# Seed stores from GpSimd's queue, and the first attention unit's key maxima by pairs with a second set of key differences

## The chip, the cores and the metric

The kernel runs on one core of a Trainium2 chip. A core has a matrix engine (PE, with its weight loads PEld), a vector engine (DVE), a scalar engine (ACT), GpSimd (POOL) and a queue engine that only issues transfers (SP), and 16 DMA engines that all queues share. The metric is the device time of one execution in microseconds, the median of several runs.

## The reference

Two independent halves, side by side in the output. Half A is a long convolution (S4D) over 2048 positions and 448 channels, with a kernel that is a sum of 256 exponentials for each channel. Half B is full softmax attention with 16 heads of 28.

```python
# A: u [1, 2048, 448]
dt = exp(log_dt);  A = -exp(log_A_real) + 1j * A_imag;  C = (C_real + 1j * C_imag) * dt[:, None]
K = 2 * real(einsum("dn,dnl->dl", C, exp((A * dt[:, None])[:, :, None] * arange(L))))
a = irfft(rfft(u_t, 2 * L) * rfft(K, 2 * L))[..., :L] + u * D_skip
# B: x [1, 2048, 448]
q, k, v = split(x @ wqkv)                       # 16 heads of 28
b = (softmax(q k^T * 28 ** -0.5) v) @ wo
out = concatenate([a, b], -1)                   # [1, 2048, 896]
```

All data is float32.

## The kernel before

**Attention.** The 16 heads are four groups (`G`) of four (`HG`), and the queries four chunks (`NQ`) of 512 (`CQ`). A unit is one group and one chunk, so there are 16. Queries and keys are split into a high and a low part, so that one product over 128 rows (four times 32) stands for a product of full precision. The projection writes these parts to DRAM: `q_d` for queries, `k_d` for keys, `v_d` for values. `load_q` brings one unit's queries back as the tile `qhat` (four loads of 32 partitions), and `load_k` one head's keys as `khat` (four loads of 32 partitions by 2048).

**The maxima.** A unit needs each query's largest score before its exponentials. `max_mm(u, i, kc)` handles one of 16 tiles `i` (a head `j` and 128 queries) in four steps `kc`, each a product of 128x512 into a PSUM tile. Step 0 multiplies with the differences `kd_g`, first half of a block of keys less the second half, for the key chunks 0 and 1; ACT takes the relu (tile `rl`). Step 1 multiplies with the second halves of these blocks, and DVE adds `rl` and takes the maximum in one operation, since max(a, b) = relu(a - b) + b. So two steps cover 1024 keys. Steps 2 and 3 multiply with key chunks 2 and 3, and DVE takes a plain maximum of 512 scores each. `max_join` takes the largest of the three parts, and `max_end` and `max_put` write the negated maxima into spare rows of `qhat`. Unit 0's maxima stand alone ahead of the main loop, with five PSUM tiles in turn (`more`). In the main loop the maxima of a later unit run beside the current unit's scores and exponentials.

**The first stage.** A list of slots `t` interleaves two things. Each call of `project` runs one projection job: 128 query or key rows of a group (`qk_proj`) or values (`v_proj`). Its evacuation follows one job later (`evac`), and for keys in chunks 0 and 1 it also makes the differences (`kb`, `dhl`) and stores them in `kd_d`. The other thing is the seeds: eight rounds `o` of `seeds(o)`, a pipeline over ACT, DVE and POOL that makes the first powers of the exponentials for half A. A round ends with two stores, `put_g` (tile `sg`, 1456 KB) and `put_e` (896 KB, in a `qhat` buffer), issued by SP. The pool of `qhat` has three buffers, for seeds and queries alike. `ahead` holds loads for the first unit by slot: from slot `A0` = 26 on the differences of group 0 (16 loads of 64 KB), and from `A1` = 34 on the queries of unit 0 (two slots, two loads each). After slot 36 (`PW` = 37) the projection's weights are released. In that space the keys of group 0 are loaded, heads 0 and 1 from ACT's queue and 2 and 3 from SP's, and then unit 1's queries and group 0's values from SP's. Then come unit 0's maxima.

**Order.** A planner orders the instructions of the first part by dependences and priorities; from the main loop on the program's order is kept. Each engine and each queue runs its own list in order. A load or store waits in its queue for its data and for its buffer, and what is behind it on that queue waits too.

**The main loop** runs 16 units of 16 steps, with half A's work in slots between. It loads the differences of later groups by `load_kd`, and the seeds by `load_sd`.

All engine instructions carry line 75 in the profile, a helper that records every operation, so the views are read by tile names.

## Time and profile before

| | us |
|---|---|
| median of three runs | 1360.99 |
| lowest and highest | 1358.85, 1361.72 |
| the profiled execution, its own time | 1363.72 |
| its span, first to last instruction | 1361.9 |
| mean granted TensorE clock | 0.976 |

Busy in that span: PE 1243.9 (91%), DVE 991.3 (73%), ACT 966.1 (71%), POOL 839.5 (62%). The DMA queues moved 205.36 MB, a mean of 151 GB/s. All of it went through SP's queue (201.13 MB) and ACT's (2.10 MB), beside 2.13 MB of instructions; POOL issued none.

A group's row in the profile reads: engine, operation, out<-in, partitions x elements, count | busy us, mean ns of one | idle us of the engine just before them, and what ended it. The chain of waits is a list of start, length and what the end depended on. A tile's row reads: engine, operation, count: shortest/median/longest ns, first and last start. SPq, ACTq stand for an engine's queue; a row of a transfer there is its issue, not its movement. A row of waits reads: who <- for whom: us in total, times, longest.

### The profile page before, as it was taken

The numbers are of one execution on the slowest core, as the hardware profiler recorded it, in microseconds if no ns is written. First come the engines' busy times: TensorE is split into PE (matmuls) and PEld (weight loads), VectorE is DVE, ScalarE is ACT, GpSimd is POOL, SyncE is SP. The second block draws the span as 40 slices with busy tenths as digits, with TensorE's granted clock in tenths as the row PEclk, the third lists the DMA queues.
The fourth block names the chain that finished last, engine by engine and source line by source line (L and its number), as shares of the span: only waits on it lengthen the run. The fifth ranks groups of instructions, "written<-read, shape, count | busy, mean of one in ns | idle before, by whom it ended". The sixth has DMA issues, their size and how long they took to land.

```text
span 1361.9 us, 33142 instructions
## 1 busy us (share of the span) xinstructions
PE 1243.9 (91%) x12625; PEld 709.8 (52%) x12625; DVE 991.3 (73%) x2138; ACT 966.1 (71%) x2067; POOL 839.5 (62%) x705
## 2 busy tenths in 40 slices
PE   6878885799999999999999999999998999998997
PEld 5657762455555555555555555555555545544433
DVE  5897886877777777777788888888887766857311
ACT  4876752488888888888888887878786655655553
POOL 3685681278877878878888988888895111202221
PEclk9988987899999999999999999999999999999999
DMA  6677669636675545378534233632325534636476
GB/s 197 199 261 266 225 212 271 179 74 150 147 164 118 128 135 159 111 202 198 162 94 97 56 73 86 146 79 67 79 65 140 189 116 161 206 111 203 138 192 176
DMA packets 200089, 205.36 MB, mean 151 GB/s; under 512 B 95993, under 2 KB 158521, under 8 KB 197881
## 3 DMA queue, kind: packets, MB, share of 16 engines
q1 hardware_dynamic: 199544, 201.13, 53.2%
q10 hardware_dynamic: 384, 2.10, 0.6%
q8 instruction: 100, 1.64, 0.5%
q14 instruction: 61, 0.49, 0.1%
HBM read 120.73 MB, written 82.18 MB: 149 GB/s over the span
## 4 chain that ended last, share of the span: by engine, by line
PE 61%; DVE 17%; ACT 12%; issue 3%; DMA 3%; POOL 3%; SPq 0%; ACTq 0%; DVEq 0%; POOLq 0%
PE pm L75 35%; PE po L75 13%; PE pss L75 12%; ACT p L75 6%; DVE mx L75 4%; DVE g L75 2%; DVE tri L75 2%; ACT rl L75 2%; DVE p L75 2%; POOL qhat L75 1%; DVE pr L75 1%; DVE zg L75 1%; DVE rl L75 1%; DVE sg L75 1%; ACT tri L75 1%
## 5 line engine op out<-in xcount | busy, mean ns | idle before, releaser
L75 ACT ACTIVATE p<-pss 128x512 f32<-128x512 f32 x1024 | 565.4, 609 | 138.5 <-PE pss L75 127.5
L75 PE MATMUL pss<-qhat,khat 128*128 128x512 f32 x1024 | 403.1, 400 | 3.3 <-ACT p L75 3.3
L75 DVE TENSOR_REDUCE mx<-pm 128x1 f32<-128x512 f32 x500 | 321.4, 683 | 116.3 <-PE pm L75 115.1
L75 PE MATMUL pm<-khat,qhat 128*128 128x512 f32 x749 | 330.1, 444 | 41.4 <-DVE mx L75 36.5
L75 POOL TENSOR_TENSOR e<-e,sdb 128x256 f32<-128x256 f32 x168 | 201.8, 1201 | 171.9 <-ACT e L75 162.9
L75 PE MATMUL po<-p,v 128*32 128x512 f32 x2048 | 271.9, 599 | 0.0
L75 POOL TENSOR_TENSOR e<-e,eu 128x256 f32<-128x256 f32 x168 | 248.1, 1477 | 13.2
L75 PEld LDWEIGHTS pm<-khat,qhat 128*128 128x128 f32 x749 | 142.0, 190 | 216.0 <-DVE mx L75 79.8
L75 PEld LDWEIGHTS pss<-qhat,khat 128*128 128x128 f32 x1024 | 191.1, 189 | 46.7 <-ACT p L75 11.2
L75 DVE CUSTOM_DVE_ANT_0 rl<-pm,rl 128x512 f32<-128x512 f32 x249 | 171.4, 688 | 48.3 <-ACT rl L75 43.8
L75 POOL TENSOR_TENSOR eu<-e,sdb 128x256 f32<-128x256 f32 x168 | 201.7, 1201 | 0.0
L75 DVE TENSOR_TENSOR g<-g,zg 128x128 f32<-128x128 f32 x392 | 162.9, 416 | 46.3 <-ACT zg L75 41.3
L75 ACT ACTIVATE rl<-pm 128x512 f32<-128x512 f32 x249 | 151.2, 607 | 20.7 <-PE pm L75 18.8
L75 POOL TENSOR_TENSOR p<-pr,pr 64x448 f32<-64x448 f32 x32 | 40.9, 1277 | 191.6 <-DVE pr L75 180.5
L75 PE MATMUL pm<-kdif,qhat 128*128 128x512 f32 x249 | 101.6, 408 | 2.2 <-DVE mx L75 1.5
L75 PEld LDWEIGHTS pm<-e,g 128*32 128x32 f32 x3584 | 63.0, 110 | 52.8 <-issue 30.8
L75 DVE TENSOR_TENSOR zg<-g,zg 128x128 f32<-128x128 f32 x224 | 87.5, 391 | 1.9
L75 PEld LDWEIGHTS po<-p,v 128*32 128x32 f32 x2048 | 56.6, 110 | 42.7 <-issue 38.0
L75 PE MATMUL pm<-xh,wh 112*128 112x512 f32 x128 | 56.8, 448 | 22.3 <-DVE hl L75 10.8
L75 PE MATMUL pm<-e,g 128*32 128x64 f32 x3584 | 72.5, 220 | 0.0
L75 ACT ACTIVATE y<-pm 128x448 f32<-128x448 f32 x48 | 26.3, 548 | 63.0 <-PE pm L75 30.7
L75 DVE TENSOR_TENSOR pr<-pm,ub 128x448 f32<-128x448 f32 x64 | 37.0, 619 | 32.7 <-PE pm L75 32.7
(137 smaller groups left out, 1571.8 us busy)
## 6 DMA issues: line engine op xcount, KB each, us to landing
sdb<-sd SPq DMA_DIRECT2D x56, 336.0 KB
qhat<-q SPq DMA_DIRECT2D x64, 256.0 KB
khat<-k SPq DMA_DIRECT2D x56, 256.0 KB
sd<-sg SPq DMA_DIRECT2D x8, 1456.0 KB
k<-hl SPq DMA_DIRECT2D x16, 512.0 KB
q<-hl SPq DMA_DIRECT2D x16, 512.0 KB
mw<-in_mw SPq DMA_DIRECT2D x16, 512.0 KB
sd<-qhat SPq DMA_DIRECT2D x8, 896.0 KB
```

The costliest lines, as they stand in the source:

```text
L75: i = f(*args, **kw)
```

## The change

- `put_e` and `put_g` are issued by GpSimd instead of SP, and so are the four loads of unit 1's queries, which moves them behind the last slot; the values' loads move there too and stay on SP.
- Unit 0's maxima run in pairs on both halves of the keys: step 2 is a product with a second set of differences (chunks 2 and 3) and a relu, step 3 the product with the second halves and the fused add and maximum. The join takes two parts instead of three. `rl` has three buffers there.
- The second differences are made in the evacuation for group 0 and chunks 2 and 3 (two jobs), stored in a new DRAM tile `kd2`, and loaded by SP (four loads of 256 KB) into a new pool `k2_p` before the keys of heads 2 and 3.
- The first differences of a group share one tile `kdif`; those of group 0 are loaded by four loads of 256 KB in slots 27 to 30, and unit 0's queries in slots 25 and 26.

Other units keep their three parts.

```diff
--- before.py
+++ after.py
@@ -41,7 +41,7 @@
 PS = 1
 SGB, XB, XL = 2, 5, 4
 K0, KP, KD, UP = 0, 3.5, 5, 3
-A0, A1 = 26, 34
+A0, A1 = 27, 25
 
 N1 = 32
 N2 = 64
@@ -103,6 +103,7 @@
     dram = ctx.enter_context(tc.tile_pool(name="dram", bufs=1, space=DRAM))
     k_d = [dram.tile([2, 128, L], F32, name=f"k_{g}") for g in range(G)]
     kd_d = [dram.tile([2, 128, CQ], F32, name=f"kd_{g}") for g in range(G)]
+    kd_d.append(dram.tile([2, 128, CQ], F32, name="kd2"))
     q_d = [[dram.tile([2, 128, CQ], F32, name=f"q_{g}_{c}") for c in range(NQ)] for g in range(G)]
     sd_d = [dram.tile([BO, 128, SDF], F32, name=f"sd_{o}") for o in range(NO)]
     yu_d = dram.tile([128, N1, D], F32, name="yu_d")
@@ -152,35 +153,42 @@
         v_g[g, c] = t = v_p.tile([128, NK // NQ, HG, 32], F32, name="v", bufs=5)
         nc.sync.dma_start(t.rearrange("p t h e -> p t (h e)"), v_d[c][:, g])
 
-    def load_kd(g, j, rows=range(4)):
-        if 0 in rows:
-            kd_g[g, j] = kd_p.tile([128, CQ], F32R, name=f"kdif{j}")
-        t = kd_g[g, j]
-        for r in rows:
-            nc.sync.dma_start(t[32 * r:32 * r + 32].bitcast(F32), kd_d[g][r % 2, 32 * j:32 * j + 32, :])
-
-    def load_q(u, rows=range(4)):
+    kd_t = kd_p.tile([128, HG, CQ], F32R, name="kdif")
+
+    def load_kd(g, j):
+        kd_g[g, j] = kd_t[:, j, :]
+        for r in range(4):
+            nc.sync.dma_start(kd_t[32 * r:32 * r + 32, j, :].bitcast(F32), kd_d[g][r % 2, 32 * j:32 * j + 32, :])
+
+    def load_kd_row(r, g=0, t=kd_t):
+
+        kd_g.update({(g, j): t[:, j, :] for j in range(HG)})
+        nc.sync.dma_start(t[32 * r:32 * r + 32].bitcast(F32), kd_d[g][r % 2].rearrange("(j p) q -> p j q", j=HG))
+
+    def load_q(u, rows=range(4), queue=nc.sync):
         g, c = divmod(u, NQ)
         if 0 in rows:
             q_u[u] = q_p.tile([128, HG, CQ], F32R, name="qhat", bufs=3)
         t = q_u[u]
         for r in rows:
-            nc.sync.dma_start(t[32 * r:32 * r + 32].bitcast(F32), q_d[g][c][r // 2].rearrange("(j p) q -> p j q", j=HG))
-
-    def max_mm(u, i, kc, ps=w_tile):
+            queue.dma_start(t[32 * r:32 * r + 32].bitcast(F32), q_d[g][c][r // 2].rearrange("(j p) q -> p j q", j=HG))
+
+    def max_mm(u, i, kc, ps=w_tile, p2=None):
+
 
         if i == 0 and kc == 0:
             m_u[u] = q_p.tile([128, HG, 4, 3], F32, name="mx", bufs=2)
         j, t = divmod(i, 4)
         pm = ps()
         q, kt = q_u[u][:, j, t * 128:(t + 1) * 128], kt_g[u // NQ][j]
-        mx = m_u[u][:, j, t, max(kc - 1, 0):max(kc - 1, 0) + 1]
-        if kc == 0:
-            nc.tensor.matmul(pm, q, kd_g[u // NQ, j], start=True, stop=True)
-            rl_u[u, i] = kd_p.tile([128, CQ], F32, name="rl", bufs=2)
+        n = kc // 2 if p2 else max(kc - 1, 0)
+        mx = m_u[u][:, j, t, n:n + 1]
+        if kc == 0 or kc == 2 and p2:
+            nc.tensor.matmul(pm, q, kd_g[G if kc else u // NQ, j], start=True, stop=True)
+            rl_u[u, i] = (p2 or kd_p).tile([128, CQ], F32, name="rl", bufs=3 if p2 else 2)
             nc.scalar.activation(rl_u[u, i], pm, AF.Relu)
-        elif kc == 1:
-            kb = kt.rearrange("p (c s n) -> p c s n", c=NQ, s=2)[:, :2, 1, :]
+        elif kc == 1 or kc == 3 and p2:
+            kb = kt.rearrange("p (c s n) -> p c s n", c=NQ, s=2)[:, kc - 1:kc + 1, 1, :]
             nc.tensor.matmul(pm.rearrange("p (c n) -> p c n", c=2), q, kb, start=True, stop=True)
             rl = rl_u.pop((u, i))
             nc.vector.tensor_tensor_reduce(rl, pm, rl, 1.0, -3.0e38, ALU.add, ALU.max, mx)
@@ -188,9 +196,9 @@
             nc.tensor.matmul(pm, q, kt[:, kc * CQ:(kc + 1) * CQ], start=True, stop=True)
             nc.vector.tensor_reduce(mx, pm, axis=AX.X, op=ALU.max)
 
-    def max_join(u):
+    def max_join(u, n=3):
         m_u[u, 1] = q_p.tile([128, HG * 4], F32, name="m1", bufs=2)
-        nc.vector.tensor_reduce(m_u[u, 1], m_u[u].rearrange("p a b c -> p (a b) c"), axis=AX.X, op=ALU.max)
+        nc.vector.tensor_reduce(m_u[u, 1], m_u[u].rearrange("p a b c -> p (a b) c")[:, :, :n], axis=AX.X, op=ALU.max)
 
     def max_end(u, ps):
         nc.tensor.transpose(ps[:16, :128], m_u[u, 1], ident)
@@ -420,8 +428,8 @@
             e8 = lambda *i: sl(q["e8"], *i)
             e3 = lambda: cmul(vec if o % 8 < E3 else pol, e8(3, 4), e8(1, 2), 1, q["e8"][:, :, 0, :, 2], q["e8"][:, :, 1, :, 2], False)
             e5 = lambda: cmul(pol, e8(5, 8), e8(1, 4), 3, q["e8"][:, :, 0, :, 4], q["e8"][:, :, 1, :, 4], False)
-            put_e = lambda: nc.sync.dma_start(sd_d[o][:, :, :F_G].rearrange("b p f -> p b f"), q["se"])
-            put_g = lambda: nc.sync.dma_start(sd_d[o][:, :, F_G:].rearrange("b p f -> p b f"), q["sg"])
+            put_e = lambda: nc.gpsimd.dma_start(sd_d[o][:, :, :F_G].rearrange("b p f -> p b f"), q["se"])
+            put_g = lambda: nc.gpsimd.dma_start(sd_d[o][:, :, F_G:].rearrange("b p f -> p b f"), q["sg"])
 
             def load():
                 if o not in nats:
@@ -463,7 +471,7 @@
                 else:
                     nc.scalar.activation(th, pp, AF.Copy)
                     nc.vector.tensor_tensor(tl, pp, th.bitcast(F32), ALU.subtract)
-                if s == 1 and c < 2:
+                if s == 1 and (c < 2 or g == 0):
                     HC = CQ // 2
                     kb = y_p.tile([128, HC], F32, name="kb")
                     dhl = y_p.tile([128, 2, HC], F32R, name="dhl")
@@ -472,7 +480,7 @@
                     nc.vector.tensor_tensor(kb, pp[:, :HC], kb, ALU.subtract)
                     nc.scalar.activation(dh, kb, AF.Copy)
                     nc.gpsimd.tensor_tensor(dl, kb, dh.bitcast(F32), ALU.subtract)
-                    nc.sync.dma_start(kd_d[g][:, :, c * HC:(c + 1) * HC].rearrange("i p l -> p i l"), dhl.bitcast(F32))
+                    nc.sync.dma_start(kd_d[g if c < 2 else G][:, :, c % 2 * HC:(c % 2 + 1) * HC].rearrange("i p l -> p i l"), dhl.bitcast(F32))
                 nc.sync.dma_start((k_d[g][:, :, c * CQ:(c + 1) * CQ] if s == 1 else q_d[g][c]).rearrange("i p l -> p i l"),
                                   hl.bitcast(F32))
             return evac
@@ -511,8 +519,8 @@
         pend, n_work = [], len(work)
 
         ahead = collections.defaultdict(list)
-        for i in range(2 * HG):
-            ahead[A0 + i].append(lambda i=i: load_kd(0, i // 2, range(2 * (i % 2), 2 * (i % 2) + 2)))
+        for i in range(4):
+            ahead[A0 + i].append(lambda i=i: load_kd_row(i))
         for i in range(2):
             ahead[A1 + i].append(lambda i=i: load_q(0, range(2 * i, 2 * i + 2)))
 
@@ -533,17 +541,22 @@
                 project()
                 wst.close()
                 k0_p = pool(k0_st, "k0_p", side="right")
+                k2_p = pool(st, "k2_p", side="right")
                 for j in range(HG):
+                    if j == 2:
+                        k2_t = k2_p.tile([128, HG, CQ], F32R, name="kd2")
+                        for r in range(4):
+                            load_kd_row(r, G, k2_t)
                     load_k(0, j, k0_p, nc.scalar if j < 2 else nc.sync)
-                load_q(1)
-                for c in range(NQ):
-                    load_v(0, c)
+        load_q(1, queue=nc.gpsimd)
+        for c in range(NQ):
+            load_v(0, c)
         xst.close()
         more = [lambda: ps_t.tile([128, CQ], F32, name="pt")] * 2 + [w_tile] * 3
         for i in range(16):
             for kc in range(4):
-                max_mm(0, i, kc, more[(4 * i + kc) % 5])
-        max_join(0)
+                max_mm(0, i, kc, more[(4 * i + kc) % 5], k2_p)
+        max_join(0, 2)
         max_end(0, ps_t.tile([128, CQ], F32, name="pt"))
         max_put(0)
         sst.close()
```

## The prediction

> **What bounds the kernel now.** I read the page's row of PE in 40 equal slices first, then busy time by stage, then the chain of waits where the stages meet. A row by stage has its length, the busy time (and instructions) of PE, its weight loads, DVE, ACT and POOL, PE's granted clock, the DMA engines' share and GB/s.
>
> ```profile
> PE   6878885799999999999999999999998999998997
> ```
>
> One digit is 34 us. Up to slice 7 (to about 264 us) PE has gaps; from there to the end it is 9 of 10 or more busy. The change edits the part ahead of that. Whatever is won or lost before about 260 us therefore moves the rest as a block.
>
> ```profile
> 0.00:204.00 204.00, 165.40 (x705) 131.31 (x705) 161.00 (x284) 134.89 (x268) 131.80 (x156) 0.92 0.69 226
> 204.00:217.85 13.85, 0.31 (x3) 0.03 (x1) 3.45 (x7) 2.22 (x6) 3.77 (x4) 0.65 1.04 288
> 217.85:251.00 33.15, 26.06 (x64) 12.81 (x64) 29.48 (x65) 9.57 (x17) 0.00 (x0) 0.89 0.96 268
> ```
>
> Three stages. Projection and seeds (0 to 204): no engine is full, PE is at 81%, DVE 79%, ACT 66%, POOL 65%. A hole (204 to 217.85): only the DMA engines work, at a share of 1.04. Unit 0's maxima (217.85 to 251): DVE is at 89% and the DMA engines still at 0.96. The chain says what ends each:
>
> ```profile
> 204.11 6.44 DMA khat<-k
> ...
> 210.93 6.78 DMA qhat<-q
> ...
> 217.85 1.19 PE pt L75 x2
> ...
> 225.82 0.60 DVE rl L75
> 226.42 1.21 DVE mx L75 x3
> ...
> 249.55 1.22 DVE mx L75 x3
> ```
>
> The hole is two loads in a row: the first key tile, and then two rows of unit 0's queries, which SP issued only when that load had landed. After it DVE repeats 0.60 (the fused add and max, `rl`) and 1.21 (two plain maxima, with the read-out of the accumulator under the first): **1.81 us for one of 16 tiles**.
>
> **The change part by part.**
>
> *Maxima in pairs.* A tile's two plain maxima are replaced by a second relu on ACT and a second fused operation on DVE.
>
> ```profile
> L75 DVE TENSOR_REDUCE mx<-pm 128x1 f32<-128x512 f32 x20 | 13.1, 685 | 11.4 <-PE pm L75 11.4
> L75 DVE CUSTOM_DVE_ANT_0 rl<-pm,rl 128x512 f32<-128x512 f32 x9 | 6.1, 681 | 1.4 <-PE pm L75 1.4
> L75 ACT ACTIVATE rl<-pm 128x512 f32<-128x512 f32 x9 | 5.4, 597 | 11.7 <-PE pm L75 9.8 <-DVE mx L75 1.9
> ...
> 221.60:242.00 20.40, 16.24 (x43) 7.07 (x42) 20.07 (x46) 6.57 (x11) 0.00 (x0) 1.00 1.05 262
> ```
>
> A fused operation lasts as long as a plain maximum (681 against 685 ns), so DVE goes from three steps of 0.60 to two, 1.21 us a tile: 16 x 0.605 = **9.7 us less**. The cover: ACT needs 2 x 0.597 = 1.19 us a tile, just under DVE; PE issues four products a tile either way and was busy 16.24 of 20.40 us at full clock over about 11 tiles, by pipelined times that overlap. So ACT follows close behind: where a relu is late, DVE waits. With PE at the lower clock it would be PE (two products took 1.19 us from 217.85 on, so four take up to 2.4). Bounds: 9.7 (DVE paces) to 0 (keys or relus pace); I take 9.7, the nearest row's.
>
> *The start.* Unit 0's queries and key differences now load during the projection, in slots 25 to 30. The 16 loads of 64 KB for the differences become four of 256 KB. The query rows leave the hole, and the second set of differences comes into it: four loads of 256 KB, of the same form as the query rows, and all four are needed before tile 0's third product.
>
> ```profile
> SPq L75 <- DMA khat<-k: 19.2, 12, 8.8
> ...
> 207.12 9.75 ACTq L75 DMA_DIRECT2D khat<-k  x5
> ...
> 211.94 0.42 SPq L75 DMA_DIRECT2D sd<-qhat  x1
> ```
>
> SP waited 8.8 us once for a load of keys that ACT had issued, though what it was to issue did not read it. The new loads stand at the same place behind the same eight, so I expect the same wait to hit them: what ends last is a different load, at the same time. Bounds: they land with the first key tile (6.8 us earlier, the query row's length), or 0.52 MB more at 288 GB/s costs 1.8 us, doubled for a shared queue 3.6. The seeds' store of 0.92 MB that SP issued at 211.94 is no longer between; I take **0**. ACT issues keys until about 216.9 in any case, and its relus stand behind them.
>
> *Second differences.* Two more evacuations make one: two copies on ACT, a subtraction on DVE and one on POOL, and a store of 256 KB.
>
> ```profile
> L75 ACT ACTIVATE kb<-pm x8: 363/374/387, 23.5 to 100.9; 128x256 f32<-128x256 f32 x8
> L75 DVE TENSOR_TENSOR kb<-pm,kb x8: 404/417/426, 24.4 to 102.3; 128x256 f32<-128x256 f32 x8
> L75 ACT ACTIVATE dhl<-kb x8: 401/416/425, 24.8 to 102.8; 128x256 fp32r<-128x256 f32 x8
> L75 POOL TENSOR_TENSOR dhl<-kb,dhl x8: 740/1168/1932, 25.3 to 106.9; 128x256 fp32r<-128x256 f32 x8
> ...
>   PE pm L75: 6.4, 4
> ```
>
> Eight of them held PE up by 6.4 us (last row: who waited for the tile), 0.8 each: **+1.6** for two. Without cover each would be 0.37 + 0.42 + 0.42 + 1.17 = 2.4, so the bounds are 0 and 4.8.
>
> *The stores on POOL's queue.* 16 of them, 896 rows each (7 blocks by 128 partitions). SP's side, then what POOL has room for:
>
> ```profile
> L75 SPq DMA_DIRECT2D sd<-qhat x8: 360/513/1276, 60.7 to 237.7; - x8
> ...
> L75 POOL TENSOR_TENSOR gz<-tri 128x224 f32<-128x224 f32 x8 | 6.8, 850 | 20.1 <-ACT tri L75 19.2 <-DVE px L75 0.8
> L75 POOL TENSOR_TENSOR vl<-tri,vh 112x448 fp32r<-112x448 f32 x4 | 5.1, 1284 | 13.0 <-ACT vh L75 9.7 <-DMA pw<-in_pw 3.2
> ...
> by line: PE pm L75 14.6%; DVE tri L75 13.4%; POOL qhat L75 9.6%; issue 6.8%; DVE sg L75 6.0%; ACT tri L75 5.8%; DVE px L75 5.7%; DVE qhat L75 5.3%; POOL tri L75 4.4%; DMA tri<-in_B_wqkv 3.9%; DVE hl L75 3.2%; PE pt L75 2.2%; POOL x_e L75 2.
> ```
>
> No row shows a DMA issued by POOL. From below: 0, all of it in POOL's idle 204 - 131.8 = 72 us. A wait for ACT's and DVE's part of a seed stands in that queue too, and behind it the next seed's products, which already idle 20.1 us before `gz` for ACT; that is its cover. From above: POOL handles one row like one element of its dearest elementwise work, 1168 ns / 256 = 4.6 ns, times 896 = 4.1 us a store, 65 us in all. The nearest row is the issue of the same store on SP; I take its longest, 1.3 us, 21 us in all. POOL stands on 9.6 + 4.4 + 2 = 16% of the chain of the first 204 us (last row), so **+3.3**.
>
> DVE's one-input operation on 128x1232 takes less time than its two-input ones:
>
> ```profile
> L75 DVE TENSOR_TENSOR tri<-tri 128x1232 f32<-128x1232 f32 x8 | 14.8, 1849 | 0.1
> L75 DVE TENSOR_SCALAR tri<-tri 128x1232 f32<-128x1232 f32 x8 | 8.8, 1096 | 0.1
> ```
>
> The Trainium skill, page "SBUF — State Buffer", section "SBUF: two separate sides", speaks against this part: while DVE runs such a faster two-port operation, POOL is locked out of the port by which it writes a DMA's descriptors. If each of the 16 stores met one, that estimate would be 16 x 1.1 = 17.6 us more on POOL, and by the same 16% the sum 2.8 us worse; no run here shows it yet.
>
> *SP relieved.* Behind SP's queue stand the stores of keys and values, whose buffers ACT waits for:
>
> ```profile
> 39.37 3.79 DMA k<-hl
> ...
> ACT hl L75 <- DMA k<-hl: 4.2, 2, 3.0
> ACT vst L75 <- DMA v<-vst: 3.8, 2, 2.8
> ```
>
> At most 8.0 us; the chain's wait for `k<-hl` lies at 39.37, before the first store of seeds (60.7), so most of it stays. I take **-1.5**, bounds 0 and -8.
>
> *The loads of unit 1's queries (to POOL's queue) and of values (later in order)* I count at 0: both are needed after 251, as now. The last seeds' stores now leave SP (236.56 and 237.74) for about 208; the first load of seeds is issued at 252.99. The cover is DMA time, and rival two takes it away.
>
> Sum: -9.7 + 0 + 1.6 + 3.3 - 1.5 = **-6.3 us**. The profiled execution took 1363.7 us (span 1361.9), so 1357.4; it lies 2.7 above the median of the runs shown (1361.0), hence **1354.7**.
>
> **The rivals.** *One, POOL becomes the bound of the first stage (slower).* Of POOL's 72 us idle, 13.0 lie before the first seed and 2.4 go to the new subtractions, so 57 are left, 3.5 us a store: that is the point from which it decides. At the upper price of 4.1 the stores need 65, 8 more than there is, and what is on the chain costs 16% of 57, or 9: -9.7 + 1.6 + 17 - 1.5 = +7.4, **1368**; every further us a store adds 16. For it: 896 rows a store and a two-step pipeline with ACT. Against it: one POOL instruction over 128x336 elements takes only about 1.0 to 1.4 us.
>
> *Two, the last keys come late (no change).* The DMA engines are full from 204 to 251. SP's order now holds back what is not urgent:
>
> ```profile
> 215.45 11.04 SPq L75 DMA_DIRECT2D khat<-k  x8
> 226.97 3.82 SPq L75 DMA_DIRECT2D qhat<-q  x4
> 231.75 3.83 SPq L75 DMA_DIRECT2D v<-v  x4
> 236.56 0.37 SPq L75 DMA_DIRECT2D sd<-sg  x1
> 237.74 0.37 SPq L75 DMA_DIRECT2D sd<-qhat  x1
> ...
> 252.99 1.04 SPq L75 DMA_DIRECT2D sdb<-sd  x2
> ...
> sd<-sg SPq DMA_DIRECT2D x8, 1456.0 KB
> sd<-qhat SPq DMA_DIRECT2D x8, 896.0 KB
> ```
>
> From POOL's queue the last seeds (2.4 MB) and unit 1's queries (1.05 MB) move beside the keys, and the second differences add 1.05 MB: 4.5 MB at 288 GB/s are up to 16 us, on keys whose issue ends at 226.5. With the last key tile at 242, four tiles and the join end at about 247 instead of 251: 3.5 us saved in place of 9.7, sum -0.1, **1361**.
>
> The Trainium skill, page "DMA: Bandwidth & Descriptors", section "Issuing engines are not separate DMA queues", has the rule behind this rival: whichever engine issues, the same 16 DMA engines carry it and interleave. The trace agrees so far as it goes: two queues together stay at 1.04 in the hole.
>
> *Three, the hole closes.* The second differences are issued with the first key tile and land with it; the maxima start near 211: 6.8 us more, **1348**. For it: SP has nothing of seeds to wait for. Against it: the 8.8 us wait on ACT's loads, and ACT's own 9.75.
>
> *Four, the pairs bring nothing*, since five PSUM buffers and ACT's relus pace a tile at 1.81 as before: +3.4, **1364**. Against it: ACT has 1.19 us of work in 1.21.
>
> **How the numbers follow.** Forecast 0.43, own range 1350 to 1359; rival one 0.22, two 0.15, three 0.15, four 0.05. 0.2% (2.7 us, about the spread of the three runs) is what can be told from no change. Faster: 0.37 of the forecast, all of three, a third of two: 0.57. Same: 0.15. Slower: one, four and the rest: 0.28. The range runs from below three (1345) to beyond one's first price (1371).
>
> **What would show it.** In unit 0's stage 32 fused operations and no plain maxima, one tile every 1.2 us, last join near 241. The start: which load ends the hole, near 218 or 211. POOL's queue in 0 to 204: DMA issues of 1.3 us; at 3.5 and more, PE's end of projection moves past 210 and the forecast is wrong. The maxima idle for `khat`: rival two. PE's wait for `kb` should be near 8 us.

## The result and the profile after

The changed kernel took 1371.07 us (median of 6 runs, 1370.21 to 1374.78), the kernel before 1362.20 (6 runs beside them): a ratio of 1.0066, 95% interval 1.0047 to 1.0084. It is slower by 6 to 11 us; 6.3 us less were forecast, with 1354.7 as the time. The profiled execution has a span of 1370.1, 8.2 more than before.

First the page's row of PE in 40 slices, then busy time by stage, with the columns of the prediction's stage rows. The first border is the end of the projection, the second the first product with the second differences, the third just behind the join of the maxima.

```profile
PE   7877692899999999999999999999998999998997
...
0.00:206.00 206.00, 163.47 (x702) 128.31 (x703) 155.59 (x272) 135.66 (x265) 137.54 (x160) 0.93 0.70 232
206.00:235.74 29.74, 3.14 (x8) 1.37 (x8) 10.40 (x22) 5.97 (x17) 14.96 (x21) 0.56 1.03 310
235.74:260.00 24.26, 21.95 (x63) 11.69 (x64) 21.15 (x65) 17.66 (x32) 0.00 (x0) 0.91 0.49 160
```

Slice 6 of PE (204 to 239 us) fell from 5 to 2: that is the hole. By the stage rows it was 13.85 us long and is 29.74. The maxima behind it got shorter, and the rest moved as a block, as forecast. The join of the maxima on DVE, before and then after:

```profile
250.79 0.20 DVE L75 TENSOR_REDUCE m<-mx 128x16 f32<-128x48 f32 x1
```

```profile
258.90 0.19 DVE L75 TENSOR_REDUCE m<-mx 128x16 f32<-128x32 f32 x1
```

From the join to the end of the span: 1361.9 - 250.8 = 1111.1 before, 1370.1 - 258.9 = 1111.2 after. So all of the loss lies ahead of 259 us, and it splits in three. The marks are the start of the projection's last product with `wl` (203.7 before, 206.3 after; one more product follows 0.2 us later in both), the start of the maxima (the first product behind which PE runs on: 217.85 before, 235.74 after) and the join:

| part | before | after | difference | forecast |
|---|---|---|---|---|
| projection, to that product | 203.7 | 206.3 | +2.6 | +3.4 (stores +3.3, evacuations +1.6, SP -1.5) |
| hole, to the start | 14.2 | 29.4 | **+15.3** | 0 |
| maxima, start to join | 32.9 | 23.2 | -9.8 | -9.7 |

The mark of the start flatters the maxima a little: by 235.74 the first pair of tile 0 had been multiplied, and DVE had done the first of its 32 operations.

The chain of waits in the hole, after (start, us, what; a tile's number is left out, so `kd<-kd` is the load of the second differences):

```profile
207.57 4.94 DMA q<-hl
...
212.62 0.61 ACT hl L75
...
213.25 0.70 DVE hl L75
...
213.97 0.36 SPq L75
...
215.86 1.56 SPq L75
...
217.46 18.23 DMA kd<-kd
...
235.74 0.80 PE pm L75
```

The projection's last evacuation waits for its buffer (the store `q<-hl`), SP sends its result off at 213.97, and only behind that in SP's list stand three of the four loads of the second differences. The last of them is issued from 217.46 on and lands 18.23 us later. PE's own record of the hole says the same, and that the first key tile came late too (224.87; it was there before 217.85 in the kernel before):

```profile
224.87 0.77 PE L75 MATMUL pt<-khat,qhat 128*128 128x512 f32 x1 [10.08 <-DMA khat<-k]
...
235.74 0.80 PE L75 MATMUL pm<-kd,qhat 128*128 128x512 f32 x1 [9.68 <-DMA kd<-kd]
```

The first key tile was late for one more reason than full engines: ACT issued one of its eight key loads at 207.20 and the other seven only from 213.09 on, behind a copy of the projection (`hl`) that waited 3.46 us for the same store `q<-hl`. Before, ACT's key loads began at 204.11 with no such gap.

What else was under way while a load of 256 KB took 18 us is in the view of the DMA queues, over the hole alone. Before, from 203.7 to 217.85 (q1 is fed by SP, q10 by ACT; packets, MB, share of the 16 engines):

```profile
DMA packets 1785, 4.10 MB, mean 290 GB/s; under 512 B 145, under 2 KB 1041, under 8 KB 1609
...
q1 hardware_dynamic: 1529, 2.65, 62.3%
q10 hardware_dynamic: 256, 1.44, 41.8%
```

After, from 206 to 235.74 (q0 is fed by POOL):

```profile
DMA packets 2897, 9.21 MB, mean 310 GB/s; under 512 B 366, under 2 KB 366, under 8 KB 2591
...
q0 software_dynamic: 1021, 4.03, 45.1%
q1 hardware_dynamic: 1521, 3.18, 37.3%
q10 hardware_dynamic: 354, 1.98, 20.1%
```

The engines are full in both. Through the longer hole go 5.11 MB more, and 4.03 MB of them are POOL's queue, which did not exist before: seeds' stores and the second unit's queries. Another 1.05 MB are the second differences. At 310 GB/s 5.11 MB take 16.5 us; the hole grew by 15.3. That agreement alone shows no cause: with the engines full in both, a longer hole carries more bytes whatever made it longer. Number 13 below is the test.

### The profile page after: what moved, and what is told of

Read it like the earlier page. It is cut to its first block, busy times and chain, and to the rows that moved or that the text cites. A ratio compares the mean times of both kernels' runs of the same rounds, so it can differ in the third digit from the quotient of the medians.

```text
span 1370.1 us, 33184 instructions
## 1 busy us (share of the span) xinstructions
PE 1240.2 (91%) x12625; PEld 706.6 (52%) x12625; DVE 984.5 (72%) x2140; ACT 979.0 (71%) x2089; POOL 857.2 (63%) x727
## 4 chain that ended last, share of the span: by engine, by line
PE 61%; DVE 14%; ACT 11%; POOL 4%; issue 4%; DMA 4%; SPq 1%; ACTq 0%; POOLq 0%
PE pm L75 35%; PE po L75 13%; PE pss L75 12%; ACT p L75 6%; DVE mx L75 3%; DVE g L75 2%; ACT rl L75 2%; POOL qhat L75 2%; DVE p L75 2%; DMA kd<-kd 1%; DVE pr L75 1%; DVE qhat L75 1%; DVE tri L75 1%; DVE zg L75 1%; PE pt L75 1%
## 5 line engine op out<-in xcount | busy, mean ns | idle before, releaser
L75 DVE TENSOR_REDUCE mx<-pm 128x1 f32<-128x512 f32 x480 | 308.4, 684 | 105.6 <-PE pm L75 104.5
L75 POOL TENSOR_TENSOR e<-e,eu 128x256 f32<-128x256 f32 x168 | 248.5, 1479 | 13.2
L75 DVE CUSTOM_DVE_ANT_0 rl<-pm,rl 128x512 f32<-128x512 f32 x259 | 178.4, 690 | 54.4 <-ACT rl L75 51.6
L75 PEld LDWEIGHTS pss<-qhat,khat 128*128 128x128 f32 x1024 | 191.2, 189 | 45.8 <-issue 11.1
L75 DVE TENSOR_TENSOR g<-g,zg 128x128 f32<-128x128 f32 x392 | 163.0, 416 | 46.4 <-ACT zg L75 41.3
L75 ACT ACTIVATE rl<-pm 128x512 f32<-128x512 f32 x259 | 156.4, 605 | 16.9 <-PE pm L75 16.0
L75 PEld LDWEIGHTS pm<-kdif,qhat 128*128 128x128 f32 x249 | 47.3, 190 | 25.5 <-DVE hl L75 7.3
```

The lines of the kernel that those rows point to most:

```text
L75: i = f(*args, **kw)
```

## The experiments

All of them, with the marks of the first 260 us read from each profile. "Hole and maxima" is the join less the projection's end; "rest" is the span less the join. The marks of a row come from one execution, the median from 4 to 12. Executions of the kernel before, run beside these, lay between 1357.3 and 1369.5 us, so a microsecond or two between two rows' marks says little. The profiled execution of number 9 is 4.5 us above its kernel's median, that of number 16 is 4.1 below.

| kernel | projection's end | join | hole and maxima | rest | median | ratio to before, 95% |
|---|---|---|---|---|---|---|
| before | 203.7 | 250.8 | 47.1 | 1111.1 | 1362.2 | |
| after | 206.3 | 258.9 | 52.6 | 1111.2 | 1371.1 | 1.0066, 1.0047 to 1.0084 |
| 1 after, no pairs | 209.1 | 256.9 | 47.8 | 1111.0 | 1370.2 | 1.0041, 1.0023 to 1.0059 |
| 2 before, pairs alone | 205.4 | 257.2 | 51.8 | 1110.1 | 1368.8 | 1.0049, 1.0026 to 1.0071 |
| 3 after, stores on SP | 214.4 | 260.3 | 45.9 | 1113.0 | 1375.1 | 1.0081, 1.0053 to 1.0109 |
| 4 before, stores on POOL | 212.6 | 265.5 | 52.9 | 1112.6 | 1379.3 | 1.0115, 1.0085 to 1.0146 |
| 5 before, stores of rounds 0 to 5 on POOL | 212.3 | 259.8 | 47.5 | 1112.9 | 1374.5 | 1.0110, 1.0062 to 1.0158 |
| 6 before, stores of rounds 6 and 7 on POOL | 203.0 | 250.0 | 47.0 | 1111.3 | 1363.6 | 1.0011, 0.9990 to 1.0032 |
| 7 before, `sd<-qhat` on POOL | 205.6 | 256.3 | 50.7 | 1110.6 | 1368.5 | 1.0028, 1.0008 to 1.0047 |
| 8 before, `sd<-sg` on POOL | 200.4 | 248.5 | 48.1 | 1110.8 | 1361.8 | 0.9987, 0.9969 to 1.0005 |
| 9 after, second unit's queries on SP | 208.1 | 258.9 | 50.8 | 1111.6 | 1367.8 | 1.0039, 1.0023 to 1.0056 |
| 10 before, queries early | 209.3 | 255.1 | 45.8 | 1111.6 | 1368.5 | 1.0052, 1.0033 to 1.0071 |
| 11 after, differences first on ACT | 204.1 | 258.4 | 54.3 | 1112.9 | 1372.7 | 1.0067, 1.0043 to 1.0091 |
| 12 before, pairs for heads 2 and 3 | 204.0 | 249.6 | 45.6 | 1113.2 | 1365.1 | 1.0009, 0.9988 to 1.0029 |
| 13 after, last stores held | 205.5 | 248.5 | 43.0 | 1118.7 | 1369.1 | 1.0044, 1.0023 to 1.0064 |
| 14 the same, differences first | 205.1 | 246.9 | 41.8 | 1121.0 | 1369.9 | 1.0048, 1.0031 to 1.0066 |
| 15 after, held, one store first | 203.8 | 247.3 | 43.5 | 1114.6 | 1362.8 | 0.9996, 0.9982 to 1.0010 |
| 16 before, last stores held | 198.1 | 240.1 | 42.0 | 1112.8 | 1358.7 | **0.9955, 0.9936 to 0.9974** |
| 17 that, with pairs for heads 2 and 3 | 203.7 | 247.1 | 43.4 | 1112.2 | 1360.1 | 0.9973, 0.9958 to 0.9988 |
| 18 that, with pairs for heads 1 to 3 | 205.5 | 251.9 | 46.4 | 1109.3 | 1362.8 | 1.0003, 0.9990 to 1.0016 |

**The pairs and their loads: 1 and 2.** One takes the pairs, the evacuations behind them and their loads out of the changed kernel; the other puts only those into the kernel before.

```diff
-                max_mm(0, i, kc, more[(4 * i + kc) % 5], k2_p)
-        max_join(0, 2)
+                max_mm(0, i, kc, more[(4 * i + kc) % 5])
+        max_join(0)
...
-                if s == 1 and (c < 2 or g == 0):
+                if s == 1 and c < 2:
...
-                    if j == 2:
-                        k2_t = k2_p.tile([128, HG, CQ], F32R, name="kd2")
-                        for r in range(4):
-                            load_kd_row(r, G, k2_t)
```

> The changed kernel without the pairs: unit 0 again takes three maxima a tile, and the second differences are neither made, stored nor loaded; stores on POOL's queue, early loads and unit 1's queries on POOL's queue stay. Theory (the second differences' loads end the hole, 18 us after their issue): the maxima start at 212 to 225 instead of 235.7, the stage takes 31 to 33 us again, time 1355 to 1364. Rival 1 (POOL's stores stretch the first stage and the last seeds): start stays at 228 or later, 1368 to 1376. Rival 2 (unit 1's queries on POOL's queue crowd the keys): start 224 to 230, 1364 to 1370.

> The kernel before with the pairs alone: second differences made, stored and loaded by SP before the keys of heads 2 and 3; seeds' stores, unit 1's queries and values on SP as before; first differences by four loads from slot 26, unit 0's queries in slots 34 and 35. Theory now (two causes: POOL's stores meet the projection's last stores in full DMA engines, and the second differences' loads stand ahead of the maxima): the start moves from 217.9 to 222 to 228 and the stage loses 9.7, so 1355 to 1363. Rival 1 (the stores on POOL are the whole loss): 1351 to 1356. Rival 2 (the loads of the second differences are the whole loss): 1368 to 1373.

Without the pairs, hole and maxima took 4.8 us less (47.8 against 52.6). With the pairs alone added to the kernel before they took 4.7 more (51.8 against 47.1). The product behind which PE runs on, in number 1 and then in number 2:

```profile
221.71 0.77 PE L75 MATMUL pt<-khat,qhat 128*128 128x512 f32 x1 [7.55 <-DMA khat<-k]
```

```profile
232.34 0.77 PE L75 MATMUL pm<-kd,qhat 128*128 128x512 f32 x1 [10.56 <-DMA kd<-kd]
```

Read with these starts, number 1 has a hole of 12.7 us (29.4 after) and maxima of 35.2 (23.2 after). Number 2 has a hole of 27.0 (14.2 before) and maxima of 24.8 (32.9 before). The two agree in kind: the pairs shorten the maxima by 8 to 12 us, and the wait for their loads makes the hole 13 to 17 us longer. 1.05 MB at 310 GB/s are only 3.4 us, so the amount of those loads alone is not the price.

Number 2 has every store of the seeds on SP, as before, and still loses 0.49%; its second rival, that the loads are the whole loss, has the time. Number 1 has no second differences, starts where its theory said (212 to 225) and still loses 0.41%; its projection ends 5.4 us later than before. So neither half of the change is free by itself.

**The stores: 3 to 8.** First all 16 back on SP in the changed kernel, then all of them, those of some rounds, or one kind, on POOL in the kernel before.

```diff
-            put_e = lambda: nc.sync.dma_start(sd_d[o][:, :, :F_G]...
-            put_g = lambda: nc.sync.dma_start(sd_d[o][:, :, F_G:]...
+            put_e = lambda: (nc.gpsimd if o < 6 else nc.sync).dma_start(sd_d[o][:, :, :F_G]...
+            put_g = lambda: (nc.gpsimd if o < 6 else nc.sync).dma_start(sd_d[o][:, :, F_G:]...
```

(Number 5; number 6 has `o > 5`, numbers 7 and 8 change one line each, number 4 both for every round.)

> The changed kernel with the 16 stores of the seeds back on SP's queue, all else as changed. Theory: the second differences still come behind the projection's last stores and through full DMA engines, so the start stays at 228 to 238, 1363 to 1374. Rival 1 (POOL's stores are the loss): start at 218 to 222, 1353 to 1358. Rival 2: 1366 to 1371, as the queries still crowd.

> The kernel before with only the 16 stores of the seeds moved to POOL's queue. Theory: 0.97 us of POOL for each and the same bytes on the DMA engines, end of projection within 3 us of before, 1360 to 1366. Rival 1: the projection ends 5 us or more later and the last seeds 10, 1367 to 1374. Rival 2: as before, 1361 to 1363.

> The kernel before with the stores of rounds 0 to 5 on POOL's queue and those of rounds 6 and 7 on SP's. With all 16 on POOL it took 1379. Theory (the harm is done where the last rounds' stores meet the projection's last stores and the keys): 1360 to 1366. Rival (the harm is done throughout, in POOL's queue): 1373 to 1380.

> The kernel before with only the stores of rounds 6 and 7 on POOL's queue. Theory: most of the 16 us of all stores on POOL, 1370 to 1379. Rival (POOL's queue throughout): 1361 to 1366.

> The kernel before, with only the eight stores sd<-qhat on GpSimd's queue (sd<-sg stays on SP). Theory (what the stores on POOL's queue cost in the kernel before is the wait of POOL's next round for the landing of sd<-qhat, whose buffer that round takes): POOL's wait for sd<-qhat 10 us or more, projection's end 208 to 212, most of the 16 us of both stores: median 1370 to 1378. Rival (the wait of the issue of sd<-sg, which stands in POOL's list until ACT's copies into sg are done, holds POOL): little here, projection's end within 2 us of 203.7, median 1361 to 1365.

> The kernel before, with only the eight stores sd<-sg on GpSimd's queue (sd<-qhat stays on SP). Theory (buffer of sd<-qhat): POOL's wait for sd<-qhat below 5 us, projection's end within 2 us of 203.7, median 1361 to 1365. Rival (POOL held at the issue of sd<-sg by ACT's copies): POOL waits for sg by 4 us or more, projection's end 207 or later, median 1367 or more.

Number 4 lies beyond all that was expected of it (1374 at most), and number 3 just beyond its theory. In number 5 and in number 6 the rival has the time, and in number 7 neither. Two ideas of mine fell here. That the last rounds' stores alone cost the time in the kernel before: number 6 has them on POOL and takes the same time. That POOL's wait for the landing of its own stores holds the first stage up: the waits of POOL for `sd<-qhat` in number 8 and in the kernel before (total, times, longest) are

```profile
POOL qhat L75 <- DMA sd<-qhat: 12.2, 4, 4.3
```

```profile
POOL qhat L75 <- DMA sd<-qhat: 1.4, 1, 1.4
```

and yet the projection of number 8 ends 3.3 us earlier. One kind of store alone moves that end by +1.9 or -3.3, both together by +8.9: the parts do not add up. The planner lists the instructions of that stage anew for every edit; numbers 4 and 8 have them in another order than the kernel before on all five engines, and numbers 13, 15 and 16 differ in order too, on PE, DVE and ACT, from the kernels that they edit. What moves the projection's end between 198 and 214 us in these kernels is not settled. In the changed kernel it moved by 2.6.

Number 3 shows something else: with the stores on SP again, hole and maxima need 45.9 us instead of 52.6, although the projection, and with it the time, is worse. The load of the second differences that ends its hole takes 12.84 us instead of 18.23, so with no store on POOL's queue it is still slow:

```profile
223.01 12.84 DMA kd<-kd
```

**The queries: 9 and 10.** The second unit's queries back on SP, behind the keys; and, in the kernel before, unit 0's queries early (`A1 = 30`) and nothing else.

```diff
-        load_q(1, queue=nc.gpsimd)
+        load_q(1)
```

> The changed kernel with unit 1's four query loads back on SP's queue (behind the keys), all else as changed. Theory: 1.05 MB less beside the second differences, at the 310 GB/s of the changed hole 3.4 us earlier, start 231 to 233, 1366 to 1369. Rival 1: no change, 1370 to 1372. Rival 2 (the queries are the loss): start 220 to 226, 1358 to 1363.

> The kernel before with unit 0's queries loaded in slots 30 and 31 instead of 34 and 35, nothing else. Theory: the hole then ends with the first key tile, start 211 to 213, 1354 to 1358. Rival 1 (ACT's queue issues keys until 217 and holds its relus): start 217 to 219, 1360 to 1363. Rival 2 (the queries take one of three buffers from the seeds, whose rounds then wait): the projection ends 4 us or more later, 1365 to 1372.

With the queries of the second unit on SP, hole and maxima are 1.8 us shorter (50.8 against 52.6), on 1.05 MB; the time is in the range of the theory, the start (235.03) is not. The early queries of unit 0 shorten hole and maxima by 1.3 us only, far from the 6.8 of the rows that left the hole: PE then waited 7.22 us for the first key tile instead. The second rival of number 10 came true: the projection ended 5.6 us later, and with it the time.

**The order of the loads: 11.** The second differences ahead of the first key tile, on ACT's queue.

```diff
+                k2_t = k2_p.tile([128, HG, CQ], F32R, name="kd2")
+                for r in range(4):
+                    load_kd_row(r, G, k2_t, nc.scalar)
                 for j in range(HG):
-                    if j == 2:
-                        k2_t = k2_p.tile([128, HG, CQ], F32R, name="kd2")
-                        for r in range(4):
-                            load_kd_row(r, G, k2_t)
```

> The changed kernel, with the four loads of the second differences ahead of the first key tile in ACT's queue instead of behind the two HW queues' other work on SP. Theory (the late start is the place of these loads: issued at 214 to 217, behind a store that waits for its projection, and 18 us under way among the key tiles): they are issued near 207 and have landed by 222, the first key tile comes 4 us later than after (near 228), so the first join of a tile starts 6 to 10 us earlier than 235.7 and the median is 1361 to 1365. Rival (the HW queues carry all loads of the hole together, and their sum of bytes sets the end, whatever the order): the start stays within 3 us of 235.7, median 1368 to 1374.

The rival has the time; PE ran on from 238.84, 3.1 us after the 235.7 of the changed kernel. The second differences were there at 220.94, but then the key tiles were late. The chain of number 11:

```profile
218.12 12.39 DMA khat<-k
230.53 8.30 DMA khat<-k
238.84 0.75 PE pm L75
```

In these two kernels what stands last waits, and the order only names what it is.

**The bytes: 13 to 16.** The four stores of rounds 6 and 7 (4704 KB) go to SP and are kept there behind the key tiles; nothing else is edited (13); the issuing engine is chosen as in number 5. One thing follows from it: the second unit's queries take a buffer that a held store reads, so they leave the hole as well. Number 14 adds the loads first on ACT's queue, and queries and values on SP behind the stores. Number 16 does the same holding in the kernel before, whose stores of round 6 stood ahead of the keys.

```diff
-                    [places, fa, e_base], [e3, g_first], [fb, e5, g_copies], [put_g], [put_e]]
+                    [places, fa, e_base], [e3, g_first], [fb, e5, g_copies]] + ([[put_g], [put_e]] if o < 6 else [[], [held.append(put_g), held.append(put_e)][:0]])
...
+                nc.kept = ("sync",)
                 k0_p = pool(k0_st, "k0_p", side="right")
...
+        for f in held:
+            f()
         load_q(1, queue=nc.gpsimd)
         for c in range(NQ):
             load_v(0, c)
+        nc.kept = KEPT["p"]
```

(`held` collects `put_g` and `put_e` of rounds 6 and 7; `nc.kept` keeps SP's list in the order of the program from there on.)

> The changed kernel, with the four stores of the seeds' rounds 6 and 7 (4.7 MB) given to SP and kept there behind the key tiles' loads; all else as in the changed kernel, the second differences' loads on SP and the second unit's queries on POOL too. Theory (the DMA engines are full from the projection's end, so the bytes ahead of the keys and of the second differences set the start; 4.7 MB at some 310 GB/s are 15 us): the second differences have landed, and the maxima's tiles run, at 222 to 228 instead of 235.7, last join 245 to 252, median 1357 to 1364. Rival (the place of the second differences' loads, in SP's list behind the projection's last stores): start within 3 us of 235.7, median 1368 to 1374.

> The same, with the second differences' loads ahead of the first key tile in ACT's queue, and the second unit's queries and the values kept on SP behind the held stores. Theory (bytes): what is left ahead of the keys are the second differences (1 MB) and the projection's last stores, so head 0 is there by 220, all keys by 232, last join 240 to 247, median 1352 to 1359: faster than both kernels. Rival (the loads of head 0 and 1 are late because ACT issues them behind four more loads, whatever else is under way): first tile near 228 and head 1 near 239 as with the second differences first alone, last join 255 or later, median 1366 to 1373.

> The kernel before, with the four stores of rounds 6 and 7 kept on SP behind the key tiles' loads (there the stores of round 6 stood ahead of them, 2.35 MB, and those of round 7 behind the values). Theory (bytes): 2.35 MB less ahead of the start are up to 7 us, of which some is not in the hole: start 211 to 215 instead of 217.9, last join 243 to 248, median 1354 to 1360. Rival (the four loads of the queries end the hole, and they wait in SP's list for the projection's last stores and for a buffer, not for bytes): start within 2 us of 217.9, median 1360 to 1366.

Number 13 is the cleanest. Its last two loads of the second differences are issued from the same microsecond on as the last one in the changed kernel, 217.45 against 217.46, and land in 6.29 us instead of 18.23 (7.5 at most, if they are what PE waited for until 224.97). Its chain of waits, and the DMA queues from 206 to 224.97, in which POOL's queue has no row:

```profile
217.45 6.29 DMA kd<-kd
...
224.97 0.76 PE pm L75
```

```profile
DMA packets 1740, 4.60 MB, mean 242 GB/s; under 512 B 219, under 2 KB 219, under 8 KB 1499
...
q1 hardware_dynamic: 1451, 3.02, 52.0%
q10 hardware_dynamic: 288, 1.57, 36.0%
```

So 11 to 12 of the 18 us go with what left the hole: the four stores and the queries. The start came at 224.97 instead of 235.74, the join 10.4 us earlier. The time did not follow, and that is the second lesson of this run: its rest is 7.5 us longer. PE's record where the main loop begins:

```profile
256.60 0.76 PE L75 MATMUL pm<-kdif,qhat 128*128 128x512 f32 x1 [7.52 <-DMA qhat<-q]
```

The second unit's queries take the buffer from which a held store reads, so POOL issues them at 244.38 and they land at 256. So start and join of number 13 are where its theory had them, and its time is in the range of its rival. Number 14, with the queries behind all four stores, waits 8.28 us there; its time, too, is in its rival's range. Number 15 puts the store of that buffer first:

```diff
-        for f in held:
-            f()
+        held[1]()
         load_q(1, queue=nc.gpsimd)
+        for i in (0, 2, 3):
+            held[i]()
```

> The changed kernel with the stores of rounds 6 and 7 held on SP behind the keys, as in the run before, but the store of round 6's qhat tile first among them, since the second unit's queries take its buffer; the queries stay on GpSimd's queue. Theory (the gain of the earlier start was given back to that one wait): start 223 to 227, last join 246 to 251, PE's wait for the queries at the head of the main loop below 2 us, median 1360 to 1365. Rival (something else holds the main loop, the values or the stores' landing): join the same, PE's wait goes to another load, median 1367 to 1371.

```profile
222.55 0.77 PE L75 MATMUL pm<-kd,qhat 128*128 128x512 f32 x1 [3.35 <-issue]
...
250.01 0.76 PE L75 MATMUL pm<-kdif,qhat 128*128 128x512 f32 x1 [2.08 <-DMA qhat<-q]
```

The wait is down from 7.52 to 2.08 us and 6.2 us of the time come with it, which puts the time in its theory's range. With these four stores held on SP, and the second unit's queries later for it, the changed kernel is level with the kernel before: 0.9996. Hole and maxima are 9.1 us shorter than after (43.5 against 52.6) and the projection ends 2.5 us earlier; the rest is 3.4 longer.

The same holding in the kernel before (16) is the fastest of all: ratio 0.9955. PE's first product with a key tile (218.41 before), and its join:

```profile
208.51 0.76 PE L75 MATMUL pt<-khat,qhat 128*128 128x512 f32 x1 [4.40 <-DMA khat<-k]
```

```profile
240.08 0.20 DVE L75 TENSOR_REDUCE m<-mx 128x16 f32<-128x48 f32 x1
```

Of the 10.7 us by which the join is earlier, 5.1 are hole and maxima, which is what the holding was expected to do, and 5.6 are an earlier end of the projection, which nobody predicted and which belongs to what is left open above; so the join lies ahead of the 243 to 248 that were expected. This execution is faster than most of its kernel: by the medians the gain is 4.9 us.

This limits what number 15 says. Held against held, the ratios are 0.9996 with the change and 0.9955 without it, so the change still costs some 0.4%. And number 6 has the same four stores on POOL's queue, without second differences, at no loss that can be told. So the stores cost time together with the second differences' loads, and they are not the whole loss.

**Pairs without the late start: 12, 17 and 18.** Pairs for the later heads only, so that their loads can stand behind the keys: in the kernel before, and with the held stores.

```diff
+                k2_t = k2_p.tile([128, 2, CQ], F32R, name="kd2")
+                for r in range(4):
+                    nc.sync.dma_start(k2_t[32 * r:32 * r + 32].bitcast(F32),
+                                      kd_d[G][r % 2, 64:].rearrange("(j p) q -> p j q", j=2))
...
-                max_mm(0, i, kc, more[(4 * i + kc) % 5])
+                max_mm(0, i, kc, more[(4 * i + kc) % 5], k2_p if i > 7 else None)
```

> The kernel before, with the keys in pairs for heads 2 and 3 alone (tiles 8 to 15): the second differences are made as in the changed kernel, but only their two last heads are loaded (four loads of 128 KB), behind all key tiles on SP's queue, so that no load of theirs stands ahead of the start. Heads 0 and 1 keep the three passes. Theory (the pairs are worth 0.6 us a tile, and only the loads ahead of the start eat it): first matmul of the maxima at 218 to 221 (the evictions of the second differences on the way cost up to 1.7 us), 8 tiles by 0.6 us less, last join start 247 to 249, median 1357 to 1360, ratio 0.996 to 0.999. Rival (any further transfers in the hole delay the key tiles as well): start at 223 or later, or head 2's tiles wait for the second differences by 4 us or more, last join at 252 or later, median 1363 to 1366.

> The kernel before with the held stores, the store of round 6's qhat tile first and the second unit's queries on GpSimd's queue, and with pairs for heads 2 and 3, their second differences loaded (0.5 MB) behind the key tiles and ahead of the held stores. Theory: start 208 to 212 as with the held stores alone (208.5), the second differences there by 222, before head 2's tiles need them near 224, last join 235 to 238 against 240.1, PE's wait for the queries below 2 us, median 1354 to 1358. Rival (the planner's order of the first stage, other in every kernel, decides more than these microseconds): projection's end off 198.1 by 4 us or more, median 1359 or more.

> The same with pairs for heads 1, 2 and 3 (0.75 MB of second differences). Theory: last join up to 2.4 us earlier than with two heads (233 to 237), less what head 1's tiles wait for the second differences, which they need near 217; median 1352 to 1357. Rival (head 1's tiles wait for the second differences, behind all keys, by 4 us or more): no gain over two heads, last join 236 or later.

In number 12 the start stayed (217.86 against 217.85), as the theory had it. Between head 1 and head 2 PE waited 1.52 us for head 2's second differences, and DVE stood for 2.51:

```profile
235.89 0.17 DVE L75 TENSOR_REDUCE m<-mx 128x8 f32<-128x24 f32 x1
238.58 0.69 DVE L75 CUSTOM_DVE_ANT_0 rl<-pt,rl 128x512 f32<-128x512 f32 x1 [2.51 <-ACT rl L75]
```

Hole and maxima lose 1.5 us, the rest gains 2.1, and the time is the same (1.0009; 1365.1 us, in the range of its rival). With the held stores, 17 is not told apart from 16 (the intervals overlap) and 18 is slower than both: the projection ended at 203.7 and 205.5, not at 198.1, and in 18 head 1's tiles waited 5.88 us for their second differences. The rivals of 17 and 18 came true. That the pairs pay in any of these places was not shown.

## Why the prediction was wrong

**The step that failed is the start.** The prediction let the second differences take the place of the query rows, "a different load, at the same time", and took 0, with bounds from -6.8 to +3.6. It was +15.3. Two things were wrong in it. The issue did not stay where it was: the query rows had been issued around the projection's last stores, the new loads stand behind the last one, which left SP at 213.97. And a load's time was taken as its own bytes, doubled at most, while the engines were full: it is the time of what is already on its way. Number 13 shows that part nearly alone, 6.29 (at most 7.5) against 18.23 us for a load issued at the same time. What is left there is the later place: its start, 224.97, is still 7.1 us behind the kernel before, 1.8 of them the projection's.

**Rival two had much of the cause and the wrong place.** It counted the stores of the last seeds, the second unit's queries and the second differences, 4.5 MB and up to 16 us, and the hole shows 5.11 MB more and 15.3 us (sizes that agree in any full hole, as said above). But it laid them on the last key tile, where four tiles would hide most, and priced 1361. They fell on the second differences and the first key tile, ahead of every tile, where nothing hides them. The rule cited there, the Trainium skill's page "DMA: Bandwidth & Descriptors", section "Issuing engines are not separate DMA queues", held: POOL's queue took 45.1% of the engines' time in the hole, and SP's and ACT's queues 37.3 and 20.1%. The cover named for the moved queries and values, "DMA time", was gone, as the text had said it might be.

**The stores on POOL's queue** were priced at 1.3 us of POOL each; the issues of the changed kernel (busy us and mean ns) are

```profile
L75 POOL DMA_DIRECT2D sd<-qhat x8 | 7.9, 982 | 2.4 <-POOL qhat L75 2.1 <-DVE sg L75 0.3
L75 POOL DMA_DIRECT2D sd<-sg x8 | 7.7, 962 | 6.4 <-ACT sg L75 4.5 <-ACT nat L75 1.9
```

so 0.97, well inside the bounds of 0 and 4.1. With that, rival one (3.5 and more) is out as it was put; the kernel is slower, but not by its mechanism. The term had nothing for the landing: POOL waited 16.2 us in all for `sd<-qhat` (1.4 before), and what that cost is not shown. The other rule cited, the Trainium skill's page "SBUF — State Buffer", section "SBUF: two separate sides", on POOL being locked out of descriptor writing while DVE runs a two-port operation, is not seen in the issues, of which none took more than 1.09 us; whether it is part of the time to landing, no run here shows. The first stage as a whole came out near its sum, +2.6 against +3.4. Numbers 4 to 8 say that this is luck as far as anything here shows: in the kernel before, the same stores moved the projection's end by +8.9, and a part of them by -3.3.

**SP relieved** was given -1.5; it can't be read apart from the same sum, and in number 3, with the stores back on SP, the projection ended 8.1 us later. That is the term's direction and the end of its bounds (-8), but with the order of the whole stage changed too. The longest wait in the chain near its end is another than the one that the term was worked out for: not a store of keys or values, but a store of seeds that SP issued. The chain of number 3:

```profile
194.59 9.89 DMA sd<-qhat
```

**The pairs** were right in kind and, by luck, in size: all 32 maxima are fused operations of 0.69 us, no plain one is left, and start to join took 9.8 us less. But a tile took 1.36 us, not 1.21 (from 242.50 to 258.17 the operations follow each other at 0.68 us, at full clock), which is 7.2 us less in 16 tiles than at 1.81. DVE was busy for 16.40 of the 17.00 us from 242 to 259, yet the chain of waits lies there at 80% on PE and at 14% on ACT, not on DVE, which was to pace it. The remainder lies in the ends of the stage: before, it took 4.0 us more than 16 x 1.81, after, 1.4 us more than 16 x 1.36, with one operation done ahead of the mark. **The evacuations** were right so far as PE shows it: its wait for `kb`, forecast near 8 us, is

```profile
PE pm L75 <- DVE kb L75: 7.5, 6, 2.5
```

**The rest as a block** was right to 0.1 us for this change; in the kernels with held stores it was not (1109.3 to 1121.0).

## What to carry to other kernels

With the DMA engines full, as in this hole, a load of 256 KB took from 6 to 18 us, by what was under way with it. So ask of a new load not only its size but what is already moving when it is issued, and whether anything there can wait. Then try the remedy on the kernel before as well: here it made that one faster too, so the change still lost. A store taken off a blocked queue is not free: the blocked queue may have been what held it behind the urgent loads. And when a stage starts earlier, read at once who waits next; here a held store kept a buffer from the next load and took back most of 10 us.

## What was not expected of the hardware

A store of 896 rows cost POOL 0.97 us to issue, against a median of 0.51 on SP for the same store. The landing, which only POOL's queue shows as a number, took far longer (KB each, us from issue to landing, over all eight and then for the two in the hole):

```profile
sd<-sg POOLq DMA_DIRECT2D x8, 1456.0 KB, 8.9
...
sd<-qhat POOLq DMA_DIRECT2D x8, 896.0 KB, 5.8
```

```profile
sd<-sg POOLq DMA_DIRECT2D x2, 1456.0 KB, 15.0
```

TensorE's granted clock falls to 0.50 in the hole and stays there into the work: the stretch 236 to 240 of the changed kernel, with PE busy throughout, was still at half speed. The kernel before shows the same on a smaller scale: 0.50 from 217.85 to 221.60.

```profile
232.00:236.00 4.00, 0.26 (x1) 0.26 (x2) 0.00 (x0) 0.00 (x0) 0.00 (x0) 0.50 1.04 343
236.00:240.00 4.00, 4.00 (x9) 2.51 (x10) 2.51 (x7) 2.53 (x5) 0.00 (x0) 0.50 1.00 342
```
